# Dealing the pieces of an output-projection weight to the DMA engines one by one

## The chip, the cores and the metric

The kernel runs on one core of one Trainium2 chip. The metric is device time in microseconds (us) of one execution; lower is better. A core has five instruction queues: PE (TensorE, matmuls and their weight loads), DVE (VectorE), ACT (ScalarE), POOL (GpSimd) and SP (SyncE, which here only issues transfers). Transfers between the chip's memory and the core's on-chip memory of 128 partitions run on sixteen DMA engines.

## The reference

A decode step for two sequences with one token each. `x` is 2x512, 32 heads of 128 attend to a cache of 4096 keys and values each, and the result is mixed with a small feed-forward block by a gate:

```python
g = sigmoid((x * gate_w).sum(-1, keepdims=True))
q = x @ wq                                        # (2, 32 heads, 128)
p = softmax(q . k_cache * 128**-0.5)              # k_cache, v_cache: (2, 32, 4096, 128), bf16
o = p . v_cache                                   # (2, 32, 128)
a = o.reshape(2, 4096) @ wo                       # wo: (4096, 512)
b = relu(x @ w1) @ w2                             # w1: (512, 1376), w2: (1376, 512)
out = g * a + (1 - g) * b
```

All inputs are bf16. The K and V caches are 64 MiB each, wq and wo 4 MiB each, w1 and w2 1.4 MB each. Nearly all of the work is reading them once.

## The kernel before

Every instruction goes into a list for its engine, in the order of the program text; each waits on counters ("markers") of the other engines and on a semaphore for each transfer. Nothing is reordered at run time: each engine, SP's issue queue among them, goes through its list in order.

**Transfers.** `kv` is one on-chip buffer with regions A, Ah, B and C. SP issues wq (into C), w1 (into B), then the K cache in 8 units of 8 MB, cut into whole units (4 MB halves side by side, 64 KB per partition) and half units (32 KB per partition), then V in the same way, each piece as soon as the region it goes to has been read by the piece before it (L281 to L284). After V come the weights for the end, in this order: the last 96 rows of w2 (semaphore `w2a`, L285), wo in two transfers (`wo0`, the first 24 KB of each partition's 32 KB, and `wo1`, the last 8 KB, L286 and L287, into region C) and the rest of w2 in three (`w2b`, `w2c`, `w2d`, L289). All of these are issued by SP and so stand in the same queue; the last thing SP issues is the store of the result.

**wo's layout.** `wo` has 4096 rows of 512; row 128h+d belongs to element d of head h. The view at L262 gives partition p the 32 rows from 32p on, one unbroken piece of 32 KB. A piece is thus a quarter of a head: piece 4h+dq holds the rows of elements 32dq to 32dq+31 of head h. A transfer over 128 partitions gives each of the sixteen DMA engines eight neighbouring partitions, so engine e reads pieces 8e to 8e+7.

**Compute.** The gate, the query projection and the first feed-forward product come first. For K, DVE transposes 32x32 blocks (L397, 64 turns) and PE takes the scores (L425 and L404). Then softmax; then for each of eleven V pieces PE multiplies (L490), DVE picks out and sums (L498, L501). `o_gather(b)` (L513) collects the head outputs of sequence b in `O_sb` (32 heads x 128) and brings them to the layout that the last product wants, with four matmuls by the 0/1 matrix `s4` (L525): partition p of `oW[:, r, b]` is to hold the element of `O_sb` that meets row r of the piece in partition p of `wreg`. `s4` is made on POOL at the start, by a clearing and one `affine_select` (L253 and L254); behind it on POOL stands only the clearing of `selx` (L257), into which DVE later writes (L318).

`project()` (L531) runs 32 matmuls on `wreg`, the first 24 behind `wo0` and the last 8 behind `wo1`. `ffn_f()` (L547) adds the rows of w2, behind `w2a` to `w2d`, and in between the projected rows; two copies on DVE, two on ACT and the store end the kernel.

Of the kernel before, what the change touches and what calls it, by code (L numbers as in the profile page):

```python
# [4 lines left out]
ALU = mybir.AluOpType  # L5
# [9 lines left out]
HALF = 16384  # L15
REGION = {"A": 0, "Ah": HALF, "B": 2 * HALF, "C": 4 * HALF}
WO_CUT = 24
# [70 lines left out]
def bass_gated_mix__gqa_block_cached__dense_activation_relu__decode_kernel(  # L88
# [33 lines left out]
    wreg = kv[:, REGION["C"]:REGION["C"] + HALF]  # L122
# [27 lines left out]
    s4 = sb("s4", [32, 4, 128], dt.bfloat16)  # L150
# [30 lines left out]
    sem = {n: nc.alloc_semaphore("sem_" + n) for n in names}  # L181
# [4 lines left out]
    def marker(name):  # L186
        m = mk.get(name)
        if m is None:
            m = _Marker()
            mk[name] = m  # L190
        return m
# [10 lines left out]
    holder = {"A": [], "Ah": [], "B": ["pe_h"], "C": ["pe_q"]}  # L202
# [15 lines left out]
    def pool(fn, waits=(), signal=None):  # L218
        P.add("pool", fn, waits=[marker(w) for w in waits], signal=marker(signal) if signal else None)
# [7 lines left out]
    def pe(fn, waits=(), signal=None, dwaits=()):  # L227
# [5 lines left out]
                                   compare_op=ALU.not_equal, fill=1.0, base=0, channel_multiplier=1),  # L233
         waits=["c_i16z"], signal="c_i16")
# [6 lines left out]
                                   compare_op=ALU.is_ge, fill=0.0, base=0, channel_multiplier=1),  # L241
         waits=["c_s1"], signal="c_s2")
    pool(lambda g: g.affine_select(out=sell_odd, in_=sell_odd, pattern=[[4, 8], [32, 4]],
                                   compare_op=ALU.is_ge, fill=0.0, base=3, channel_multiplier=-1),
         waits=["c_s2"], signal="c_sell")
    pool(lambda g: g.memset(mask8[:], 1.0), signal="c_m1")
    pool(lambda g: g.affine_select(out=mask8[:], in_=mask8[:], pattern=[[-16, 8]],
                                   compare_op=ALU.is_ge, fill=0.0, base=0, channel_multiplier=1),
         waits=["c_m1"], signal="c_m2")
    pool(lambda g: g.affine_select(out=mask8[:], in_=mask8[:], pattern=[[16, 8]],  # L250
                                   compare_op=ALU.is_ge, fill=0.0, base=15, channel_multiplier=-1),
         waits=["c_m2"], signal="c_mask8")
    pool(lambda g: g.memset(s4[:], 0.0), signal="c_s4z")  # L253
    pool(lambda g: g.affine_select(out=s4[:], in_=s4[:], pattern=[[1, 4], [-1, 128]],  # L254
                                   compare_op=ALU.not_equal, fill=1.0, base=0, channel_multiplier=4),
         waits=["c_s4z"], signal="c_s4")
    pool(lambda g: g.memset(selx[:], 0.0), signal="c_selx")  # L257


    wq_in = A_wq.rearrange("(p t) n -> p (t n)", t=4)  # L260
    w1_in = B_w1.rearrange("(p t) f -> p (t f)", t=4)
    wo_in = A_wo.rearrange("(p r) n -> p (r n)", r=32)  # L262
    w2a_in = B_w2[0:1280, :].rearrange("(p r) n -> p r n", r=10)
    k_rows = A_k_cache.rearrange("b h s d -> (b h s) d")
    v_rows = A_v_cache.rearrange("b h s d -> (b h s) d")
# [8 lines left out]
    def sp(fn, waits=(), dwaits=()):  # L274
        P.add("sp", fn, waits=waits, dwaits=dwaits)
# [5 lines left out]
    for kind, n, u, halves, region in pieces:  # L281
        sp(lambda e, kind=kind, u=u, halves=halves, region=region:
           e.dma_start(piece_sb(halves, region), piece_in(kind, u, halves)).then_inc(sem_region[region], 16),
           waits=[marker(m) for m in predecessor[kind, n]])  # L284
    sp(lambda e: e.dma_start(w2[0:96, 10, :], B_w2[1280:1376, :]).then_inc(sem["w2a"], 16), waits=[marker(holder["B"][0])])  # L285
    sp(lambda e: e.dma_start(wreg[:, 0:512 * WO_CUT], wo_in[:, 0:512 * WO_CUT]).then_inc(sem["wo0"], 16), waits=[marker(holder["C"][0])])  # L286
    sp(lambda e: e.dma_start(wreg[:, 512 * WO_CUT:HALF], wo_in[:, 512 * WO_CUT:HALF]).then_inc(sem["wo1"], 16))  # L287
    for name, r0, r1 in (("w2b", 0, 4), ("w2c", 4, 9), ("w2d", 9, 10)):
        sp(lambda e, name=name, r0=r0, r1=r1: e.dma_start(w2[:, r0:r1, :], w2a_in[:, r0:r1, :]).then_inc(sem[name], 16))  # L289
    sp(lambda e: e.dma_start(out.rearrange("b s n -> (b s) n"), out_sb[:, :]).then_inc(sem["out"], 16),  # L290
# [333 lines left out]
```

## Time and profile before

| | |
|---|---|
| median of 3 runs | 345.46 us (345.19 to 345.66) |
| profiled execution: its time | 345.01 us |
| profiled execution: its span, first to last instruction | 343.50 us |
| mean granted TensorE clock in it | 0.839 |
| read from memory | 145.43 MB, 423 GB/s over the span |
| wo0 (3072 KB): issue to landing | 24.0 us |
| wo1 (1024 KB): issue to landing | 26.1 us |
| w2b, w2c, w2d (512, 640, 128 KB): issue to landing | 26.9, 28.0, 27.9 us |

The span is one profiled execution, from the first instruction to the last; the execution's own time is 1.51 us more, for what lies around the span. "Issue to landing" contains the time that a transfer stands in the queue behind others. In lines of the profile, `kv<-in_A_wo_dram` is a transfer of wo into `kv`, and an instruction line gives its source line as L and a number; `PEld` is PE's loading of weights, and a `q` behind an engine's name means its queue of issues.

### The profile page before, as it was taken

Reading aid. Unit: us, or ns where it says so; the run is one execution under the profiler, and the core shown is the slowest. Engines: PE = TensorE matmul, PEld = TensorE weight load, DVE = VectorE, ACT = ScalarE, POOL = GpSimd, SP = SyncE. Lnnn points to the kernel's source line nnn. Section 1 sums busy time; section 2 is a strip of 40 time slices with the busy share of each in tenths; the row PEclk is TensorE's granted clock in tenths of the full one; section 3 lists DMA queues with packets and bytes.
Section 4 is the critical chain, followed back from the end, with each engine's and each line's share of the span. In section 5 each row is a group of like instructions: output and inputs, shape, how many; then the busy total and the mean of one; then the engine's idle time right before and its main releaser. Section 6 shows DMA issues by size and latency. Waiting matters only on the chain.

```text
span 343.5 us, 2507 instructions
## 1 busy us (share of the span) xinstructions
PE 198.0 (58%) x1232; PEld 54.0 (16%) x976; DVE 192.2 (56%) x137; ACT 14.8 (4%) x54; POOL 7.7 (2%) x20
## 2 busy tenths in 40 slices
PE   0440497998797996988999275016055042262463
PEld 0240011111111111111111032002022010021131
DVE  0400698996997996989999596303024103031122
ACT  1040001010001001000000300000000000000000
POOL 8000000000000000000000000000000000000000
PEclk9999999999899999899999858556578556566669
DMA  7998989999999989999999989999999989999995
GB/s 313 462 488 368 481 374 427 458 450 466 391 427 427 481 383 466 406 404 443 443 477 401 467 382 473 406 443 427 397 467 420 473 389 473 393 425 427 425 387 239
DMA packets 4163, 145.57 MB, mean 424 GB/s; under 512 B 469, under 2 KB 698, under 8 KB 954
## 3 DMA queue, kind: packets, MB, share of 16 engines
q1 hardware_dynamic: 4148, 145.43, 98.5%
q8 instruction: 8, 0.13, 0.2%
q14 instruction: 1, 0.01, 0.0%
q10 hardware_dynamic: 6, 0.00, 0.0%
HBM read 145.43 MB, written 0.00 MB: 423 GB/s over the span
## 4 chain that ended last, share of the span: by engine, by line
DMA 75%; DVE 16%; PE 7%; issue 1%; ACT 0%; SPq 0%; DVEq 0%
DMA kv<-in_A_v_cache_dram 35%; DMA kv<-in_A_k_cache_dram 28%; DVE kt L397 16%; DMA kv<-in_B_w_dram 8%; DMA kv<-in_A_wq_dram 4%; PE PS L490 3%; PE PS L425 1%; PE PS L404 1%; PE PS L338 1%; PE PS L377 1%; ACT qrow L351 0%; PE PS L357 0%; PE PS L543 0%; DVE out_sb L563 0%; SPq L287 0%
## 5 line engine op out<-in xcount | busy, mean ns | idle before, releaser
L397 DVE STREAM_TRANSPOSE kt<-kv 128x2048 f32<-128x2048 f32 x64 | 141.1, 2274 | 24.4 <-DMA kv<-in_A_k_cache_dram 24.4
L425 PE MATMUL PS<-kt,qbuf 128*128 128x512 bf16 x256 | 105.7, 413 | 34.1 <-DVE kt L397 28.5
L404 PE MATMUL PS<-kt,qbuf 128*128 128x512 bf16 x256 | 105.2, 411 | 0.0
L490 PE MATMUL PS<-kv,kt 128*32 128x512 bf16 x512 | 48.7, 560 | 89.7 <-DMA kv<-in_A_v_cache_dram 80.9
L498 DVE TENSOR_TENSOR qbuf<-PS,maskc 128x512 f32<-128x512 f32 x11 | 7.6, 691 | 95.5 <-PE PS L490 95.5
L425 PEld LDWEIGHTS PS<-kt,qbuf 128*128 128x128 bf16 x256 | 25.4, 99 | 142.2 <-DVE kt L397 74.4
L490 PEld LDWEIGHTS PS<-kv,kt 128*32 128x32 bf16 x512 | 18.6, 132 | 118.6 <-issue 70.2
L472 DVE TENSOR_TENSOR kt<-kt,mask 128x512 bf16<-128x512 bf16 (+1 forms) x17 | 19.3, 1181 | 0.0
L333 ACT ACTIVATE qbuf<-PS 32x4 bf16<-32x4 bf16 (+1 forms) x40 | 7.6, 190 | 108.4 <-PE PS L404 106.8
L501 DVE TENSOR_REDUCE qbuf<-qbuf 128x128 f32<-128x512 f32 x11 | 11.2, 1021 | 0.4
L565 ACT ACTIVATE out_sb<-PS 2x128 bf16<-2x128 f32 x2 | 0.5, 271 | 145.0 <-PE PS L543 145.0
L338 PE MATMUL PS<-kv,xTw 128*32 128x512 bf16 x32 | 3.6, 631 | 3.1 <-DMA kv<-in_A_wq_dram 3.1
L445 ACT ACTIVATE kt<-PS,negm 128x512 bf16<-128x512 f32 x4 | 2.7, 686 | 58.9 <-DVE negm L441 58.9
L297 PE MATMUL PS<-ident,x_sb 3*128 3x3 bf16 x4 | 0.3, 165 | 7.9 <-DMA x_sb<-in_gate_w_dram 7.9
L300 DVE COPY xT<-PS 128x12 bf16<-128x12 bf16 x1 | 0.2, 170 | 8.2 <-PE PS L297 8.2
L354 DVE CAST qrow<-PS 128x256 bf16<-128x256 f32 x2 | 2.4, 1396 | 3.8 <-PE PS L338 3.8
L236 POOL MEMSET qbuf<- 128x5120 bf16 x1 | 4.4, 4358 | 0.0
L433 DVE TENSOR_REDUCE mpad<-PS 128x2 f32<-128x2048 f32 x1 | 2.3, 2291 | 2.2 <-PE PS L404 2.2
L517 PE MATMUL PS<-qbuf,selx 128*32 128x128 f32 x22 | 3.0, 276 | 0.8 <-DVE qbuf L501 0.8
L449 DVE STREAM_TRANSPOSE kt<-kt 128x1024 bf16<-128x1024 bf16 x2 | 2.5, 1245 | 1.6 <-ACT kt L445 1.5
L383 DVE TENSOR_SCALAR hT<-PS,gm 128x10 bf16<-128x10 f32 x2 | 0.5, 227 | 5.0 <-PE PS L377 5.0
L536 PE MATMUL PS<-kv,oW 128*2 128x512 bf16 x32 | 2.1, 378 | 2.0 <-DMA kv<-in_A_wo_dram 2.0
(62 smaller groups left out, 32.5 us busy)
## 6 DMA issues: line engine op xcount, KB each, us to landing
kv<-in_A_v_cache_dram SPq DMA_DIRECT2D x6, 4096.0 KB, 37.6
kv<-in_A_k_cache_dram SPq DMA_DIRECT2D x4, 4096.0 KB, 31.6
kv<-in_A_wq_dram SPq DMA_DIRECT2D x1, 4096.0 KB, 12.1
kv<-in_A_wo_dram SPq DMA_DIRECT2D x1, 3072.0 KB, 24.0
kv<-in_B_w_dram SPq DMA_DIRECT2D x1, 1376.0 KB, 15.0
kv<-in_A_wo_dram SPq DMA_DIRECT2D x1, 1024.0 KB, 26.1
kv<-in_B_w_dram SPq DMA_DIRECT2D x1, 640.0 KB, 28.0
kv<-in_B_w_dram SPq DMA_DIRECT2D x1, 512.0 KB, 26.9
```

The lines of the kernel that those rows point to most:

```text
L236: pool(lambda g: g.memset(qbuf[:], 0.0), signal="c_qbuf")
L333: act(lambda a: a.activation(out=out, in_=src, func=ACT.Copy), waits=waits, signal=f"q_{b}_{u}_{blk}_{par}")
L338: pe(lambda e, n=n, t=t: e.matmul(psf(32 * (n % 4), 32 * (n % 4) + 32, (QR_B + n // 4) * BANK, 512), lhsT=xTw[:, t, :], rhs=wreg[:, t * 40 ...
L377: return e.matmul(psf(0, m, H_C0 + 2 * ft, 2), lhsT=cols, rhs=xT3[:, t, 0:2], start=(t == 0), stop=(t == 3))
L397: dve(lambda v: v.transpose(out=dst, in_=pairs[:, h, 64 * a:64 * a + 64, :]), waits=([f"pe_sc_{i - NKT}"] if i >= NKT else []), dwaits=([l ...
L404: return e.add_instruction(mybir.InstMatmult(start_tensor_calc=start, stop_tensor_calc=stop, tile_size=(128, 128), tile_position=(0, 0), l ...
L425: return e.matmul(out, lhsT=lhsT, rhs=rhs, start=start, stop=stop)
L472: dve(lambda v: v.tensor_tensor(out=out, in0=src.unsqueeze(2).to_broadcast(shape), in1=mask8[:].unsqueeze(1).unsqueeze(3).to_broadcast(sha ...
L490: pe(lambda e, j=j, t=t: e.matmul(psf(32 * t, 32 * t + 32, V_BS[n % 2] * BANK, 512), lhsT=v_weights(n)[:, j], rhs=rows[:, :, j, :], start= ...
L498: dve(lambda e: e.tensor_tensor(out=parts, in0=psf(0, 128, V_BS[n % 2] * BANK, 512).rearrange("p (c d) -> p c d", c=4), in1=maskc[:].unsqu ...
L501: dve(lambda e: e.tensor_reduce(out=X2[:, b, k, :], in_=parts.rearrange("p c d -> p d c"), axis=AX.X, op=ALU.add), waits=[f"dve_m{n}"], si ...
L517: pe(lambda e, n=n, w0=w0: e.matmul(psf(0, 32, O_C0, 128), lhsT=selx[:, w0:w0 + 32], rhs=X2[:, b, n - mine[0], :], start=(n == mine[0]), s ...
```

## The change

The view of wo takes the pieces in another order: partition 8e+t gets piece 16t+e, so the engine that fills partitions 8e to 8e+7 reads every sixteenth piece, and the sixteen engines together read sixteen neighbouring pieces at a time. The source pattern of the two transfers has three levels (16 engines, 8 pieces, the bytes) in place of two. Since the piece in a partition is another one, `s4` follows: for head h = 4t+l and quarter dq the one stands at partition 32l+8dq+t. It is built with four `affine_select` instructions, one for each dq, on a view of 4x4x8 elements, in place of one on 512. Nothing else differs.

```diff
     pool(lambda g: g.memset(s4[:], 0.0), signal="c_s4z")
-    pool(lambda g: g.affine_select(out=s4[:], in_=s4[:], pattern=[[1, 4], [-1, 128]],
-                                   compare_op=ALU.not_equal, fill=1.0, base=0, channel_multiplier=4),
-         waits=["c_s4z"], signal="c_s4")
+    for dq in range(4):
+        view = s4[:, dq, :].rearrange("h (l q t) -> h l q t", l=4, q=4)
+        pool(lambda g, view=view, dq=dq: g.affine_select(out=view, in_=view, pattern=[[-1, 4], [-100, 4], [-4, 8]],
+                                                         compare_op=ALU.not_equal, fill=1.0, base=100 * dq, channel_multiplier=1),
+             waits=["c_s4z"], signal=("c_s4" if dq == 3 else None))
     pool(lambda g: g.memset(selx[:], 0.0), signal="c_selx")
...
-    wo_in = A_wo.rearrange("(p r) n -> p (r n)", r=32)
+    wo_in = A_wo.rearrange("(t e r) n -> e t (r n)", e=16, r=32)
...
-    sp(lambda e: e.dma_start(wreg[:, 0:512 * WO_CUT], wo_in[:, 0:512 * WO_CUT]).then_inc(sem["wo0"], 16), waits=[marker(holder["C"][0])])
-    sp(lambda e: e.dma_start(wreg[:, 512 * WO_CUT:HALF], wo_in[:, 512 * WO_CUT:HALF]).then_inc(sem["wo1"], 16))
+    sp(lambda e: e.dma_start(wreg[:, 0:512 * WO_CUT], wo_in[:, :, 0:512 * WO_CUT]).then_inc(sem["wo0"], 16), waits=[marker(holder["C"][0])])
+    sp(lambda e: e.dma_start(wreg[:, 512 * WO_CUT:HALF], wo_in[:, :, 512 * WO_CUT:HALF]).then_inc(sem["wo1"], 16))
```

## The prediction

> **What bounds the kernel now.** I read the page first, then the end of the chain of waits, then busy time by stretch around wo, then the timeline at the start and around the issue of wo, and last the trace's packet records (start, length and size of every DMA packet) and its landings (the sixteen increments that each transfer's semaphore gets).
>
> The page's busy line, the slices of DMA, its queue and the chain:
>
> ```profile
> PE 198.0 (58%) x1232; PEld 54.0 (16%) x976; DVE 192.2 (56%) x137; ACT 14.8 (4%) x54; POOL 7.7 (2%) x20
> ...
> DMA  7998989999999989999999989999999989999995
> ...
> q1 hardware_dynamic: 4148, 145.43, 98.5%
> ...
> DMA 75%; DVE 16%; PE 7%; issue 1%; ACT 0%; SPq 0%; DVEq 0%
> ```
>
> No compute engine is over 58% busy, and SP's queue keeps the sixteen DMA engines occupied for 98.5% of the span. DVE's 16% of the chain is in the K stage, where a transfer waits for a region; the DMA slices stay at 8 and 9 there, because another transfer is queued. The kernel reads 145 MB and lasts about as long as that takes.
>
> The chain from 305 us on, start, length, what:
>
> ```profile
> 311.69 0.34 SPq L286
> ...
> 313.03 28.01 DMA kv<-in_B_w_dram
> 341.04 0.04 issue
> 341.08 0.59 PE PS L543 x24
> ```
>
> The last thing waited for is w2, issued at 313 and landed at 341 although it is small: it stands in the same queue behind the rest of V and behind wo. So a microsecond more or less on wo is one on the end. Behind w2 there is a fixed tail: twenty-four matmuls, two copies, the store.
>
> Busy time by stretch; the last two columns are the share of DMA time and GB/s:
>
> ```profile
> 316.00:325.20 9.20, 3.51 (x32) 1.27 (x32) 1.71 (x2) 0.00 (x0) 0.00 (x0) 0.69 1.00 428
> 325.20:329.20 4.00, 1.00 (x12) 0.53 (x16) 0.00 (x0) 0.00 (x0) 0.00 (x0) 0.50 1.01 385
> 329.20:333.60 4.40, 3.66 (x38) 1.92 (x26) 1.71 (x2) 0.00 (x0) 0.00 (x0) 0.72 0.99 417
> ```
>
> The first row is V, the second the small w2a (96 runs of 1 KB) and the first packets of wo, the third wo alone. In the second the engines are as busy but move less: packets take longer there. That is the one soft place near the change.
>
> The packet records give the sizes. A run is one packet: 65,536 bytes take 2.419 us, 32,768 take 1.215, wo's 24,576 take 0.915 and its 8,192 take 0.311 (medians): 27.1, 27.0, 26.8 and 26.2 GB/s on one engine. The best wo packets are already near the best of the run. In the second row 24 KB packets take up to 1.172, and the last V packets up to 1.475. The landings of w2a run from 326.13 to 328.38 and those of wo1 from 336.17 to 338.21: wo takes 10.04 us on the earliest engine and 9.83 on the latest. About half the engines are some 1.5 us behind; the queue of instruction loads has eight 16 KB packets of about 1.05 us, spread from 27.81 to 331.90, and the number of late landings grows after each. The change touches none of that.
>
> **The change part by part.** Timeline rows: start, length, queue and line:
>
> ```profile
> 8.30 0.62 POOL L254 TENSOR_SCALAR_AFFINE_SELECT s<-s 32x512 bf16<-32x512 bf16 x1
> 8.88 0.15 POOL L257 MEMSET selx<- 128x56 f32 x1
> ...
> 10.78 0.28 DVE L318 TENSOR_REDUCE selx<-ident 128x8 f32<-128x128 bf16 x1
> ...
> 311.69 0.34 SPq L286 DMA_DIRECT2D kv<-in_A_wo_dram  x1
> 312.08 0.43 SPq L287 DMA_DIRECT2D kv<-in_A_wo_dram  x1
> 312.55 1.38 SPq L289 DMA_DIRECT2D kv<-in_B_w_dram  x3
> ```
>
> The selection matrix: one affine_select of 512 elements a row (0.62 us) becomes four of 128. The trace has such selects of 128 elements (0.29, L232) and of 8 (0.20, L247), so four cost 0.80 to 1.16, which is 0.18 to 0.54 us more on POOL. Only the clearing of selx is queued behind; it would end at 9.21 to 9.57 instead of 9.03. DVE's reduction into selx starts at 10.78, held by its own earlier work, so at least 1.2 us of cover is left. Without that cover DVE would start up to 0.54 late, and its next work on the path waits for wq, whose matmuls begin at 12.93. The matrix itself is read at 334.53. Cost: nothing. The four matmuls that permute the output (L525) keep their number and shapes.
>
> SP's issue (0.34 and 0.43 us, then 1.38 for w2's three): wo's two transfers now have a source pattern of three levels instead of two. The trace has no such pattern on SP. Its issues of a whole tensor take 0.34 to 0.46 us, the longest of any transfer 0.53 (ACT). Even at 1 us more for each, wo0 is taken up by the engines at 325.46, 13 us after its issue, and wo1 and w2's pieces at 333 and later. The V transfers ahead cover it. Cost: nothing; without cover it would be the same 1 or 2 us.
>
> The reads: the same 4 MB in the same 128 runs of 24 KB and 128 of 8 KB, eight of each for every engine, to the same partitions. What moves is where the engines read at one time: 256 KB apart before, 32 KB apart after, and an engine's successive runs lie 512 KB apart instead of 32 KB. Eight packets at 0.915 and eight at 0.311 make 9.81 us: against 10.04 the most that wo itself can give is 0.23, and with the excess of the last V packets (up to 0.26, if wo's first reads cause it) about 0.45 in all. From the other side, every packet like the slowest 24 KB one (1.172 against 0.915, or 28%) would make it 2.75 us longer. The rows nearest to the new pattern are mixed: K's and V's engines are 512 KB apart, w1's 86 KB, w2b to w2d 80 KB, and all run undisturbed (4,096-byte packets take 0.160); only w2a's engines, 6 KB apart, fall together with a slow stretch. 32 KB lies between, and nearer in ratio to 80 than to 6, so I take no cost: 0, with -0.45 and +2.75 kept as ends.
>
> The longer jump inside an engine: a 32 KB V packet, with a jump of 64 KB to its next, takes 5.5 ns more than half a 64 KB one; sixteen such jumps cost 0.09 us, twice the fixed part of a packet (13 ns, from the line through 24 and 64 KB) 0.2. I put in 0.05. [...] No row here has that step within an engine; with 512 KB between engines K's packets ran at full rate.
>
> Sum against the profiled execution: 345.01 (span 343.50 and 1.51 around it) + 0 + 0 + 0.05. The median of the runs is 0.45 higher, 345.46, which gives 345.5.
>
> **The rivals.**
> *Neighbours collide (slower).* Sixteen engines in one stretch of 512 KB crowd one part of the memory. For it: the stretch at 385 GB/s begins with reads packed into 96 KB, and slows V packets on other engines too. Against it: w2a is also the only transfer of 96 partitions with 1 KB runs, and 80 KB between engines did no harm. At 385 instead of 428 GB/s 4.19 MB take 10.89 instead of 9.80 us: +1.1, or 346.6; at the slowest packet +2.75, or 348.2. It decides from 7% on wo: 24 KB packets of 0.98 instead of 0.915.
>
> *The soft place goes (a little faster).* If wo's starts 256 KB apart make it, the new order removes it: -0.2 to -0.45, or 345.0 to 345.3. For it: slow packets start as wo does. Against it: wq has the same layout and its second to eighth packets run at 1.211 to 1.213, apart from two. Even whole it stays below what can be told apart.
>
> *The pattern is dealt otherwise.* Three levels might go out in smaller packets or to fewer engines. 4 KB packets (0.160 each) would cost 0.96 for 24 KB, 5% or 0.5 us; eight engines would cost 10 us more. [...]
>
> **How the numbers follow.** A measurement here can tell about 0.2%, 0.69 us, from no change. [...] The soft place goes: 0.12, of which 0.02 beyond 0.69. Neighbours collide: 0.33. Dealt otherwise, or an instruction load falling on an engine that is already late (one such load is worth the 1.5 us of lateness): 0.09. A gain from what no row shows: 0.10. So faster 0.12, same 0.46, slower 0.42. The range runs from 344.8 (below the soft place's 345.0 by the runs' spread of 0.2) to 348.2; the likeliest case alone is 345.2 to 345.8.
>
> **What would show it.** Right: 24 KB packets at 0.915 and wo1's last landing near 338.2 after w2a's near 328.4; the slow stretch unchanged; POOL's selx at 9.1 to 9.4 and DVE's unmoved. Wrong: packets above 0.98 all through wo (neighbours), packets near 0.915 from the first one (the soft place gone), other sizes or unequal landings (dealt otherwise), or a change ahead of 325 us, which nothing here explains.

## The result and the profile after

The change makes the kernel slower: 356.20 us median (355.82 to 356.59) against 345.39 (345.15 to 345.66) on the same chip, a ratio of 1.0313 with a 95% interval of 1.0302 to 1.0324. That is 10.8 us, about four times the most that the prediction had allowed for. The profiled execution took 356.32 us, its span 354.9.

The page of the changed kernel, the lines that answer to those shown of before (busy time, DMA by slices, the queue, the chain):

```profile
PE 201.0 (57%) x1232; PEld 55.0 (16%) x976; DVE 192.1 (54%) x137; ACT 14.8 (4%) x54; POOL 8.6 (2%) x23
...
DMA  8999899999899999999999899999999999999995
GB/s 336 414 473 467 362 465 417 417 465 473 364 406 502 392 458 451 393 403 458 425 465 452 380 462 452 406 436 425 415 447 465 406 428 414 430 421 379 209 206 164
...
DMA 75%; DVE 12%; PE 10%; issue 1%; SPq 1%; ACT 0%; DVEq 0%
```

The same line of GB/s of the kernel before:

```profile
GB/s 313 462 488 368 481 374 427 458 450 466 391 427 427 481 383 466 406 404 443 443 477 401 467 382 473 406 443 427 397 467 420 473 389 473 393 425 427 425 387 239
```

The busy shares would lead nowhere: the DMA engines are as occupied as before, to the end. The line of GB/s tells it. Up to slice 36 it runs at some 430 as before. In slices 38 and 39, which wo fills, it stands at 209 and 206; the last, 164, also holds the rest of w2 and the tail. The engines are busy and move half as much.

Busy time by stretch, the two stretches around wo's start; the last columns are the DMA share and GB/s:

```profile
325.20:329.20 4.00, 0.00 (x0) 0.00 (x0) 0.00 (x0) 0.00 (x0) 0.00 (x0) 0.59 1.07 224
329.20:333.60 4.40, 2.76 (x28) 1.27 (x32) 0.00 (x0) 0.00 (x0) 0.00 (x0) 0.50 0.98 202
```

Before, these were 385 and 417. The packet records give the same for single packets: the sizes and counts have not changed (128 of 24,576 bytes, 128 of 8,192), but their medians are 1.889 and 0.559 us instead of 0.916 and 0.313.

The timeline on POOL, and on SP around the issue of wo:

```profile
8.30 1.48 POOL L256 TENSOR_SCALAR_AFFINE_SELECT s<-s 32x128 bf16<-32x128 bf16 x4
9.74 0.14 POOL L259 MEMSET selx<- 128x56 f32 x1
...
312.46 0.63 SPq L288 DMA_DIRECT2D kv<-in_A_wo_dram  x1
313.13 0.59 SPq L289 DMA_DIRECT2D kv<-in_A_wo_dram  x1
```

The four selects take 1.48 us together, and the two issues 0.63 and 0.59 where they took 0.34 and 0.43. Both are covered: DVE writes selx at 10.57, and the engines come to wo at 325.97.

The end of the chain:

```profile
314.40 37.81 DMA kv<-in_B_w_dram
352.20 0.04 issue
352.25 0.84 PE PS L545 x24
```

Where the time went in the two profiled executions, from the last landing of each transfer (before, after): w2a 328.38 and 331.04, wo1 338.21 and 349.57, w2d 341.38 and 352.53. So 2.66 us are lost before the end of w2a. That fits engines that are late and still bring V while the early ones are already at wo: w2a's first eight landings come by 327.01, the other eight from 328.82 to 331.04, and the last V packets take up to 2.385 us instead of 1.475. Another 8.70 are lost on wo itself (18.53 instead of 9.83 on the latest engine), and 0.21 come back on w2. The sum is 11.15. The span grew by 11.4; the matmuls at the very end take 0.84 instead of 0.59 us, at a granted clock of 0.50 instead of 1.00, which is the other quarter.

### The profile page after: what moved, and what is told of

It reads as the page before. It is cut to its first block, busy times and chain, and to the rows that moved or that the text cites. A ratio compares the mean times of both kernels' runs of the same rounds, so it can differ in the third digit from the quotient of the medians.

```text
span 354.9 us, 2513 instructions
## 1 busy us (share of the span) xinstructions
PE 201.0 (57%) x1232; PEld 55.0 (16%) x976; DVE 192.1 (54%) x137; ACT 14.8 (4%) x54; POOL 8.6 (2%) x23
## 4 chain that ended last, share of the span: by engine, by line
DMA 75%; DVE 12%; PE 10%; issue 1%; SPq 1%; ACT 0%; DVEq 0%
DMA kv<-in_A_v_cache_dram 34%; DMA kv<-in_A_k_cache_dram 27%; DVE kt L399 12%; DMA kv<-in_B_w_dram 11%; DMA kv<-in_A_wq_dram 3%; PE PS L492 3%; PE PS L427 3%; PE PS L406 3%; PE PS L340 1%; PE PS L379 1%; ACT qrow L353 0%; PE PS L545 0%; SPq L288 0%; PE PS L359 0%; SPq L291 0%
## 5 line engine op out<-in xcount | busy, mean ns | idle before, releaser
L492 PE MATMUL PS<-kv,kt 128*32 128x512 bf16 x512 | 47.7, 549 | 93.0 <-DMA kv<-in_A_v_cache_dram 84.3
L538 PE MATMUL PS<-kv,oW 128*2 128x512 bf16 x32 | 3.8, 620 | 9.4 <-DMA kv<-in_A_wo_dram 9.4
L519 PE MATMUL PS<-qbuf,selx 128*32 128x128 f32 x22 | 4.4, 378 | 0.0
L519 PEld LDWEIGHTS PS<-qbuf,selx 128*32 128x32 f32 x22 | 3.5, 164 | 1.7 <-issue 1.0
```

The lines of the kernel that those rows point to most:

```text
L492: pe(lambda e, j=j, t=t: e.matmul(psf(32 * t, 32 * t + 32, V_BS[n % 2] * BANK, 512), lhsT=v_weights(n)[:, j], rhs=rows[:, :, j, :], start= ...
L519: pe(lambda e, n=n, w0=w0: e.matmul(psf(0, 32, O_C0, 128), lhsT=selx[:, w0:w0 + 32], rhs=X2[:, b, n - mine[0], :], start=(n == mine[0]), s ...
L538: pe(lambda e, r=r, t=t: e.matmul(psf(32 * t, 32 * t + 2, PR_C0, 512), lhsT=oW[:, r, :], rhs=wreg[:, r * 512:(r + 1) * 512], start=(r < 4) ...
```

## The experiments

The prediction had three explanations for a slowdown: the engines read too close to each other, an engine's runs lie too far apart, or the transfer is dealt otherwise. A fourth comes with the issue of 0.63 us: the way of issue. The first runs tell them apart.

In the expectations, read theory and jump theory are the first two of these. Dealing theory is the third: what counts is which partitions the engines write at one time. Which partitions then hold each other up it leaves open; y3_phases and y4_more_sets put that to the test. "Another reason" is a reason other than the partitions. "Plain eighths" means eight neighbouring partitions for each engine, in order.

**The same reads, three levels.** Partitions 8e to 8e+7 get pieces 8e to 8e+7 back, in reverse, so that the source keeps three levels; s4 follows.

```diff
-    wo_in = A_wo.rearrange("(t e r) n -> e t (r n)", e=16, r=32)
+    wo_in = bass.AP(A_wo.tensor, 7 * HALF, [[8 * HALF, 16], [-HALF, 8], [1, HALF]])
```

> wo's source pattern has three levels as in the change, but partition 8e+t gets piece 8e+7-t: if a transfer gives each engine eight neighbouring partitions, every engine reads the same eight pieces as before, last first, 256 KB from the next engine. s4 follows. Read theory (the change is slow because sixteen engines read 32 KB apart): back to the time before, 345.4 us, 24 KB packets at 0.915 us. Jump theory (slow because an engine's runs lie 512 KB apart): also 345.4. Dealing theory (slow because with three levels the transfer is cut into plain eighths of the partitions, so that two engines write through the same way into the partitions at one time, which a transfer of two levels avoids): as slow as the change, 356 us, 24 KB packets at 1.9 us. [...]

Measured: 355.87 us, ratio 1.031 (1.028 to 1.034); 24 KB packets at 1.890. SP's issues took 0.63 and 0.59 us, as in the change.

**Close reads, two levels.**

```diff
-    wo_in = A_wo.rearrange("(p r) n -> p (r n)", r=32)
+    wo_in = bass.AP(A_wo.tensor, 0, [[HALF // 4, 128], [1, HALF]])
```

> wo's source keeps two levels, but successive partitions read 24 KB and 8 KB runs that start only 8 KB apart (they overlap; the projected rows are not those of wo, everything else is). All reads of the sixteen engines lie within 1 MB, with engines 32 or 64 KB apart. Read theory: at least as slow as the change, 356 us or more, 24 KB packets at 1.9 us or more. Jump theory and dealing theory: 345.4 us, packets at 0.915.

Measured: 345.23 us against 345.22, ratio 1.0005 (0.9993 to 1.0016); packets at 0.916. Stretch 329.2 to 333.6 of the two runs, first the reversed neighbours, then the close reads:

```profile
329.20:333.60 4.40, 4.01 (x41) 2.30 (x42) 0.69 (x1) 0.00 (x0) 0.00 (x0) 0.64 0.94 201
```

```profile
329.20:333.60 4.40, 3.88 (x41) 2.08 (x30) 1.51 (x2) 0.00 (x0) 0.00 (x0) 0.72 0.96 408
```

The two answer each other: reads 256 KB apart with three levels are slow (packets at 1.890), and reads that all lie within 1 MB, with two levels, are not (0.916). Where the engines read does not matter here; neither a gain nor a loss hangs on it.

**The longer issue, by itself.** The kernel before, its two transfers of wo marked for the longer issue path (`nc.dge_precook = False` around them).

> The kernel before, but wo's two transfers are issued in the longer way that a three-level pattern needs (SP was busy 0.63 and 0.59 us with them in the change, 0.34 and 0.43 before); pattern, pieces and partitions are as before. If the way of issue by itself makes the transfer slow: 356 us, packets at 1.9 us. Read, jump and dealing theory (which needs the three levels): 345.4 us, packets at 0.915.

Measured: 345.05 us, ratio 0.9997 (0.9986 to 1.0008), packets at 0.916, though SP was busy 1.16 us with the two issues. The way of issue costs nothing.

**Sixteen neighbouring partitions at a time.**

```diff
-    sp(... dma_start(wreg[:, 0:512 * WO_CUT], wo_in[:, 0:512 * WO_CUT]) ...)      # and wo1
+    wo_in = A_wo.rearrange("(e j r) n -> j e (r n)", e=16, r=32)
+    for cut in (first 24 KB, last 8 KB): for j in range(8):
+        sp(... dma_start(wreg[16 * j:16 * j + 16, cut], wo_in[j, :, cut]) ...)
```

> wo goes in sixteen transfers of sixteen neighbouring partitions with two levels each; at one time the engines read pieces 256 KB apart (piece 8e+j to partition 16j+e), an engine's successive pieces are 32 KB apart, and s4 follows. SP needs about 6.5 us for the issues, from 311.7 to 318, and the engines come to wo at 325.5, so the issue costs nothing. Read theory and jump theory: 345.4 us. [...]

Measured: 364.92 us, ratio 1.0573 (1.0515 to 1.0631), packets at 2.55, the slowest at 3.03. Two levels, the short issue (7.25 us for all sixteen) and reads 256 KB apart, and still the slowest of all: what is left is the partitions that are written at one time, or the sixteen transfers in place of two, which the next run tells apart.

**Partitions 8 apart, and 7 apart.** The same sixteen transfers to `wreg[j:j+121:8]`, and to `wreg[j:j+106:7]` with partitions 112 to 127 as an eighth group.

> wo in sixteen transfers of sixteen partitions again, but with partitions 8 apart (the j-th goes to partitions j, 8+j, ... 120+j), each partition its own piece as before: reads 256 KB apart, two levels, one partition for each engine. [...] If transfers of sixteen partitions are slow for another reason (their number, one run for each engine): as x4_sixteen, 2.55 us and 364.9.

> As x8_step8, but seven transfers to partitions 7 apart (j, 7+j, ... 105+j) and the eighth to partitions 112 to 127; reads 224 KB apart. [...] Another reason for slow transfers of sixteen partitions: 2.55 us and 364.9, or as x8_step8.

Measured: 356.53 us (1.0334, 1.0315 to 1.0353), packets at 1.874; and 356.52 us (1.0334, 1.0315 to 1.0352), packets at 1.707. The first is the dealing that the theory gives to the change, written out by hand, and it gives the change's time (356.20) and packet (1.889). With as many transfers as x4_sixteen it is 8.4 us faster, so the partitions matter. The second was expected to be faster, on an estimate that no run here bears out; it takes as long, with shorter packets. Whether that comes from its sets of partitions or from engines that work on different sets at one time, these two runs do not tell; the next two take sets one by one.

**The cost by itself.** Groups of transfers to chosen partitions, each alone. This kernel and the next ran once each; their groups are compared within the run.

```diff
+    sets = [slice(32, 93, 4), slice(11, 117, 7), slice(0, 121, 8), slice(0, 16),
+            slice(0, 29, 4), slice(48, 77, 4), slice(0, 57, 8), slice(0, 8)]
+    for i, part in enumerate(sets):
+        for r in ("C", "A", "Ah", "B"):
+            sp(... dma_start(kv[part, REGION[r]:REGION[r] + HALF], wo_in[part, :]) ...)
+        sp(lambda e, i=i: e.wait_ge(sem["wo1"], 64 * (i + 1)))
+    # then all of wo with three levels, and all of wo with two
```

> The disputed cost by itself. Once V has been read, SP issues in place of wo's two transfers one group of transfers after the other, each group alone (SP waits for its landing): four 32 KB runs per partition to a chosen set of partitions, one partition for each engine. In order: (1) 32, 36, ... 92; (2) 11, 18, ... 116; (3) 0, 8, ... 120; (4) 0 to 15; then on eight engines only (5) 0, 4, ... 28; (6) 48, 52, ... 76; (7) 0, 8, ... 56; (8) 0 to 7; last all of wo with the change's three levels (9) and all of wo with two levels as before (10), which the rest of the kernel uses. The time of the whole kernel says nothing; the 32 KB packets do. [...] If a transfer of few partitions is slow as such: (1) and (5) are slow too.

Busy time by stretch, one row for each of the groups (1) to (10); the last column is GB/s:

```profile
332.60:339.60 7.00, 0.67 (x6) 0.30 (x6) 1.50 (x4) 0.00 (x0) 0.00 (x0) 0.85 0.83 300
341.20:348.10 6.90, 0.00 (x0) 0.00 (x0) 0.00 (x0) 0.00 (x0) 0.00 (x0) 0.50 0.80 290
349.60:360.20 10.60, 0.00 (x0) 0.00 (x0) 0.00 (x0) 0.00 (x0) 0.00 (x0) 0.50 0.94 198
361.90:380.60 18.70, 0.00 (x0) 0.00 (x0) 0.00 (x0) 0.00 (x0) 0.00 (x0) 0.50 0.98 112
383.30:389.40 6.10, 0.00 (x0) 0.00 (x0) 0.00 (x0) 0.00 (x0) 0.00 (x0) 0.50 0.46 172
391.10:397.20 6.10, 0.00 (x0) 0.00 (x0) 0.00 (x0) 0.00 (x0) 0.00 (x0) 0.50 0.45 172
398.80:408.90 10.10, 0.00 (x0) 0.00 (x0) 0.00 (x0) 0.00 (x0) 0.00 (x0) 0.50 0.48 104
410.70:429.20 18.50, 0.00 (x0) 0.00 (x0) 0.00 (x0) 0.00 (x0) 0.00 (x0) 0.50 0.49 57
432.00:452.20 20.20, 0.00 (x0) 0.00 (x0) 0.00 (x0) 0.00 (x0) 0.00 (x0) 0.50 0.98 208
453.90:465.00 11.10, 0.00 (x0) 0.00 (x0) 0.00 (x0) 0.00 (x0) 0.00 (x0) 0.50 0.99 402
```

| group | partitions written at one time | median 32 KB packet, us |
|---|---|---|
| (1) | 32, 36 ... 92 | 1.21 |
| (2) | 11, 18 ... 116 | 1.22 |
| (3) | 0, 8 ... 120 | 2.56 |
| (4) | 0 to 15 | 4.82 |
| (5), (6) eight engines | 0, 4 ... 28 and 48, 52 ... 76 | 1.30, 1.25 |
| (7) eight engines | 0, 8 ... 56 | 2.56 |
| (8) eight engines | 0 to 7 | 4.82 |
| (9) all of wo, three levels | not shown | 2.57 |
| (10) all of wo, two levels | not shown | 1.21 |

The packet takes about one, two or four times 1.21 with the set of partitions. (7) and (8) are as slow with eight engines as (3) and (4) with sixteen, so it is not the number of engines; (1), (2), (5) and (6) are fast, so transfers of few partitions are not slow as such. (In the fast groups the first packets are longer, up to 2.5 us; the GB/s of the short groups contain that.) And (9) beside (10), the same bytes to the same partitions one after the other, is the change: 208 against 402 GB/s.

**More sets.** What made x9_step7 slow, engines out of step (on different sets at one time) or its sets themselves, and what other shapes do.

```diff
+    for part in [slice(j, j + 106, 7) for j in range(7)]:  # four runs of 32 KB each, as above
+    for n in (96, 64, 32): alone([(wreg[0:n, :], wo_in[0:n, :])])
+    two = kv[:, 0:4 * HALF].rearrange("p (g m) -> p g m", g=2)[:, :, 0:HALF // 2]
+    alone([(two, bass.AP(A_wo.tensor, 0, [[HALF, 128], [HALF // 2 - 1024, 2], [1, HALF // 2]]))])
```

> As y3_phases, other groups, each alone: (1) to (7) x9_step7's first seven sets one by one, partitions j, 7+j, ... 105+j, four 32 KB runs each; (8) pieces to partitions 0 to 95, (9) 0 to 63, (10) 0 to 31, one transfer of two levels each; (11) three levels with 128 outermost on both sides: two runs of 16 KB to each of 128 partitions (read 14 KB apart); (12) all of wo with two levels, which the rest uses. The time of the whole kernel says nothing. [...]

Rows for groups (1) and (4), and for (8) to (11):

```profile
333.30:343.30 10.00, 0.67 (x6) 0.30 (x6) 1.47 (x4) 0.00 (x0) 0.00 (x0) 0.61 0.94 210
...
369.40:379.00 9.60, 0.00 (x0) 0.00 (x0) 0.00 (x0) 0.00 (x0) 0.00 (x0) 0.50 0.65 218
...
417.50:433.00 15.50, 0.00 (x0) 0.00 (x0) 0.00 (x0) 0.00 (x0) 0.00 (x0) 0.50 0.91 203
434.60:445.20 10.60, 0.00 (x0) 0.00 (x0) 0.00 (x0) 0.00 (x0) 0.00 (x0) 0.50 0.96 198
446.90:452.60 5.70, 0.00 (x0) 0.00 (x0) 0.00 (x0) 0.00 (x0) 0.00 (x0) 0.50 0.84 184
454.20:465.40 11.20, 0.00 (x0) 0.00 (x0) 0.00 (x0) 0.00 (x0) 0.00 (x0) 0.50 0.93 374
```

The explanation by engines out of step falls: five of the seven sets are slow alone. Groups (4) and (5) are mostly fast: three quarters of the packets take 1.85 or less, with medians of 1.30 and 1.21, and the slowest tenth 2.4. In the other five all sixteen engines are slow: medians of 2.44 to 2.50. The landings say the same: in group (4) two come at 379.9 and all others by 377.64, while in group (1) the last sixteen landings all fall between 342.96 and 343.92. All seven sets have steps of 7 and differ only in where they begin. Why five of them are slow and two are not, no run here shows.

Transfers over 96, 64 and 32 partitions run at 203, 198 and 184 GB/s, about half of the 402 of (10) in y3_phases. Group (11) is fast: its 16 KB packets take 0.61. So a third level by itself does no harm; an outermost level of 16 does (24 KB packets at 1.889 in the change, 1.890 in x1_back_step).

**The last rows of w2 over all partitions.** The 96-partition transfer of the kernel before, w2a, is one of these shapes, and may make the slow stretch before wo.

```diff
-    sp(... dma_start(w2[0:96, 10, :], B_w2[1280:1376, :]) ...)
+    sp(... dma_start(w2[:, 10, :], B_w2[1248:1376, :]) ...)
+    # the product's last block takes hidden rows 1248 to 1375; hT[0:32, 10, :] is cleared
```

> The kernel before, but the last rows of w2 go over all 128 partitions: rows 1248 to 1375, of which the first 32 are read twice and meet zeros in hT (one more memset on DVE, 0.15 us early on). 32 KB more are read, 0.08 us. [...] If the slow stretch comes from wo's first reads instead: it stays, and the time is 345.3, 0.1 more than before.

Measured: 344.80 us against 345.05, ratio 0.9992 with an interval of 0.9983 to 1.0001, which just reaches 1. The trace is clear, though. The stretch that had 385 GB/s before:

```profile
325.20:329.20 4.00, 1.31 (x16) 0.60 (x20) 0.00 (x0) 0.00 (x0) 0.00 (x0) 0.53 0.99 412
```

The last V packets take at most 1.221 us instead of 1.475, and 24 KB packets at most 0.955, apart from one beside an instruction load (1.380, as before). So the soft place comes from w2a's 96 partitions, not from where wo's reads start. That its writes collide with the packets around it fits the slow 96-partition transfer (8) above; no run takes it apart further. What it is worth in the kernel's time, 0.25 us, is at the edge of what these runs can tell.

**Reads 512 KB apart.**

```diff
-    wo_in = A_wo.rearrange("(p r) n -> p (r n)", r=32)
+    wo_in = bass.AP(A_k_cache.tensor, 0, [[16 * HALF, 128], [1, HALF]])
```

> The kernel before, but in place of wo the same number of bytes is read from the K cache, two levels, 128 runs that lie 512 KB apart (the projected rows are not those of wo). Read theory has nothing against it; jump theory: every run of an engine is 512 KB from its last, so 24 KB packets at 1.9 us and 356 us. [...] Dealing theory: 345.2, packets at 0.915.

Measured: 345.07 us against 345.05, ratio 1.0001 (0.9991 to 1.0010), packets at 0.918. Jump theory falls: at this step nothing is lost that can be seen, and the packets are 0.2% longer than the 0.916 of before.

## Why the prediction was wrong

*What bounds the kernel* held: the stream of the DMA engines sets the end, a microsecond on wo is one on the end, and the added POOL and SP work was covered (1.48 us on POOL was more than the 1.16 forecast and selx was cleared at 9.88, still before DVE's start at 10.57; the issues of 0.63 and 0.59 stood behind 13 us of V). Two small readings were off and change nothing: the medians before are 0.916 and 0.313, so eight of each make 9.83, not 9.81, and with 0.26 on V the most to gain is 0.47, not 0.45.

*The reads* is the step that failed, in its sentence "the same 4 MB in the same 128 runs ..., eight of each for every engine, to the same partitions. What moves is where the engines read at one time". The partitions as a whole are the same; which are written at one time is not. I took it that an engine has eight neighbouring partitions before and after, and so looked at the read side alone. For the unchanged transfer that is not so: x8_step8 writes out just this dealing with two levels and takes 356.53 us, with packets at 1.874 where the unchanged ones take 0.916, and group (3) of y3_phases takes 2.56 where (10) takes 1.21. The change itself behaves like those two. So the sum has no term for the writes, and they cost some 11 us (8.70 and 2.66). From there the ends of the range came from the wrong rows: -0.45 to +2.75, where it was +8.7 on wo and +2.7 on what runs beside it.

*The rival with the right name* was "the pattern is dealt otherwise", and it had the wrong mechanism: smaller packets or fewer engines. All sixteen engines took part (sixteen landings for each of wo's transfers, a DMA share of 0.98) in packets of the same size. That its "10 us more" for eight engines comes near the 10.8 measured is luck. What the runs show in its place is the set of partitions: 8 apart, as plain eighths write them, packets take twice as long (x8_step8; (3) of y3_phases), and so does the whole of wo with three levels ((9) beside (10), 2.57 and 1.21). How the unchanged transfer is dealt, partition by partition, and so how far apart its engines read, no run here shows: its full rate (0.916 against 1.874 for the 24 KB packets) excludes only plain eighths.

*Neighbours collide* had a chance of 0.33 and the right direction, but by reads that are close together; x1_back_step is slow without them (355.87 us) and x2_close_reads is fast with them (345.23). *The soft place goes* named the wrong cause: it is w2a, by x6_w2_full, whose median is 0.25 us lower, of the 0.45 that I had put as the most. The row that I read against it, "w2a is also the only transfer of 96 partitions", was the one to follow.

*The longer jump* costs nothing that can be seen: x3_far_steps, at 512 KB, is 0.02 us from before. The likeliest case, with a chance of 0.36, allowed for a cost of this jump in its upper end, 345.8; no run shows that term.

*What would show it* held in one point: packets above 0.98 all through wo were to mean neighbours. They came, and meant something else; the sign did not tell the two apart.

## What to carry to other kernels

When a transfer's pattern changes, ask not only where it reads but which engine writes which partitions at the same moment: on this chip a transfer with 128 partitions outermost on both sides ran at full rate (402 GB/s), and the same bytes with an outermost 16 (208), or transfers over 96, 64 or 32 partitions (203, 198, 184), at about half of it. A small transfer of such a shape slowed the packets around it too (the last V packets took up to 1.475 us, and 1.221 once it was filled up to 128 partitions), so fill it up where that is cheap. And a DMA share of 1.0 is no sign that the rate holds: read GB/s beside it, and the time of one packet of a known size.

## What the runs showed of the hardware

- The time of a 32 KB packet went with the set of partitions written at one time: 1.21 to 1.30 us for four sets with steps of 4 or 7, 2.56 with steps of 8 from 0 on, 4.82 for neighbours from 0 on, the last two alike with sixteen engines and with eight.
- Of seven other sets with steps of 7, five held up all sixteen engines (medians of 2.44 to 2.50 us) and two were mostly fast (medians of 1.30 and 1.21, in one of them two landings late). Why they differ stays open.
- Reads of sixteen engines within 1 MB, or in runs 512 KB apart, went at the rate of before (24 KB in 0.916 and 0.918 us; before, 0.916).
- An issue by SP of a wo transfer took 0.34 to 0.43 us with two levels over all partitions, 0.59 to 0.63 with three levels, and 0.63 with two levels and partitions 8 apart (10.03 for sixteen). Behind 13 us of queue the longer form cost nothing (345.05 us, ratio 0.9997).
